# W_out's feature tiles half as seven block products, wider early weight fetches, buffers cleared by VectorE

## The chip, the cores and the metric

The kernel runs on one core of a Trainium2 chip. The core has a TensorE (matrix products, PE in the rows), a VectorE (DVE), a ScalarE (ACT), a GpSimd (POOL) and a SyncE (SP) that issues the DMA transfers. What is measured is the device time of one execution in microseconds (us); the kernel before takes 538.59 us in the median of three runs.

## The reference

Three parts follow each other: causal attention, a gated feed-forward layer with a root-mean-square norm ahead of it, and a bilinear layer.

```python
# q, k, v: (2, 12, 448, 64); x: (896, 768) after attention
scores = scale * np.matmul(q, k.transpose(0, 1, 3, 2))     # causal mask, then softmax
attn_out = np.matmul(attn, v)
...
rms = np.sqrt(np.mean(x * x, axis=-1, keepdims=True) + 1e-06)
xn = x / rms * rms_g
g = xn @ w_gate                                            # 768 -> 1536
val = xn @ w_val                                           # 768 -> 1536
x = g * (1.0 / (1.0 + np.exp(-g))) * val @ w_out           # 1536 -> 768
...
a = x @ w1                                                 # 768 -> 1024
b = x @ w2
h = a * b @ w3                                             # 1024 -> 1024
out = h @ w_out                                            # 1024 -> 768
```

## The kernel before

Everything is held with features on the 128 partitions and the 448 tokens of one batch row along the free axis. A float32 operand is split into a 16-bit high part and a 16-bit low part, and a product is three matmuls: high by high, high by low, low by high. So every product of a 128 by 128 weight tile with 448 tokens is three matmuls of 448 columns.

The weights come as 64-bit words. `fetch` issues the DMA on SyncE, unpacks the word with three passes (L462 on VectorE, L465 on ScalarE or L467 on VectorE, L469 on VectorE), and `halve` makes the high part (L445 on ScalarE or L446 on VectorE) and the low part (L449 on VectorE). `load_w` is both.

The last two weights are independent of the tokens and are multiplied first: `w_prime` computes W' = w3 times the last w_out, in matmuls of 384 columns, while the attention runs. It fetches w_out in pieces 384 columns wide and w3 in pieces 512 wide.

Most later products use a seven-product scheme for two-by-two blocks (Strassen-Winograd): the two batch rows of tokens are one block axis, two halves of the output or input features the other. `unit` prepares a weight's seven block combinations (two fetches of 768, four sums by VectorE, the halves), `mix` the seven combinations of the activations (`part` makes the two halves of one), and `wino` runs the seven products through PSUM banks, with three copies between banks by ScalarE (`fork`, L859) and two sums by VectorE (`join`, L864). The gate stage has 12 such groups (one for each feature tile f of 1536), the w1/w2 stage 8, the last stage 3.

W_out, between gate and w1/w2, is not done in this way: for each of the six output tiles d and each batch row, 12 feature tiles times three matmuls go into one bank, 432 matmuls of 448 columns in all, and its weight comes in 12 fetches of 768 columns.

```python
        for b in range(B):
            pr = T2 + (q + b / 2) * step
            ps, kp = mm_b.next()
            terms = []
            for f in range(NF):
```

The order of all instructions is decided before they are issued. `Plan.add` notes each piece of work with its engine, an estimated duration, what it reads and writes and a priority; `Plan.schedule` places the pieces on a timeline, and `Plan.order` issues them in the order of that timeline. The priorities are sums of the constants at the top (TP, WP0, WPS, GVS, OS, AS, FS and the table PO). Where that timeline leaves TensorE idle by more than 0.3 us in its first 50 us, pairs of matmuls with no use are put in, called fillers here (L435, 252 columns each). Each engine runs its own list in order and waits for the others by semaphores.

At the start VectorE clears `zero` (which the fillers read), and GpSimd clears and fills the masks (`masks`) and then the identity, the pads of `vh`, `pB` and `tB` (`pads`).

Of the kernel before, what the change touches and what calls it, by code (L numbers as in the profile page):

```python
# [18 lines left out]
P = 128  # L19
# [21 lines left out]
TP = 28.2101  # L41
WP0 = -128.5418
WPS = 43.0076
GVS = -29.6299
OS = -20.1067
AS = 4.781
FS = -7.5297
PO = dict(dq=-213.4192, dv=276.1722, vh=102.5046, vl=144.5046, sc=-0.1481, s3=-108.5638, hA=-122.7468,
    hl=86.4469, hB=-304.4551, pv=217.9082, sq=148.6883, nm=50.454, wm=-18.9366, ww=44.0488, wx=446.4336,
    g=314.9881, a=147.5041, o=-146.2756, f=300.9707, gm=162.7087, e=-116.3983, ae=122.9146, y=214.6087,  # L50
    t1=120.1752, mx=-49.7567, fk=-118.0695, pm=373.8229, dw=68.9952)
# [9 lines left out]
ARENA = 177152  # L61
# [177 lines left out]
LAT = {"pe": 0.25, "sp": 2.6, "dve": 0.12, "act": 0.12, "pool": 0.12}  # L239
# [32 lines left out]
def dma_us(b):  # L272
    return b / 335.0e3 + 0.1
# [3 lines left out]
def fused_kernel(ctx: ExitStack, tc, qk, v, g, wgv, wo, wab, w3t, wout, out):  # L277
# [61 lines left out]
    early = Ring("att", "se", 6, [P, 512, 2], I32), Ring("att", "ce", 6, [P, 512], I32)  # L339
# [37 lines left out]
    ew_r = Ring("late", "ew", 5, [P, S], F32)  # L377
    kp_r = Ring("late", "kp", 6, [P, S], F32)
    un = []
    for r in range(3):  # L380
        if r == 2:
# [3 lines left out]
          for f in range(NF) for b in range(B) for j in range(2)}  # L385
    wo_r = Ring("late", "wo", 3, [P, 2, DF], F16, [(j, c) for j in range(2) for c in range(2)])
# [12 lines left out]

    def abset(s, i, j):  # L400
        return ab[s, i, j], ("ab", s, i, j)

    def masks():
        nc.gpsimd.memset(mask, 0.0)
# [4 lines left out]
        nc.gpsimd.memset(mask3, 0.0)  # L409
# [6 lines left out]

    def pads():
        nc.gpsimd.memset(mhalf, -0.5)
        nc.gpsimd.memset(ident, 0.0)
# [4 lines left out]
        for t in vh_r.tiles:  # L424
            nc.gpsimd.memset(t[:, :, D:D + 1], 1.0)
        for i in range(2):
            nc.gpsimd.memset(pB_r.tiles[i][:, S:], 0.0)
            nc.gpsimd.memset(tB_r.tiles[i][:, :, :, 128:192], 0.0)

    add("pool", 2.5, masks, w=["mask"], prio=-10)  # L430
    add("pool", 1.6, pads, w=["mhalf", "ident"] + [(n, i) for n in ("vh", "pB", "tB") for i in range(2)], prio=1)

# [8 lines left out]
    add("dve", 0.54, lambda: nc.vector.memset(zero, 0.0), w=["zero"], prio=-10)  # L441
# [9 lines left out]

    def fetch(src, n, prio, rings=(st_r, cv_r)):
# [3 lines left out]
        (st, ks), (cv, kc) = (r.next() for r in rings)  # L456
# [4 lines left out]
            out=st, in_=src.bitcast(I32).rearrange("p (n t) -> p n t", t=2)), w=[ks], prio=prio + PO["dw"])  # L461
# [29 lines left out]
    def third(it, c, prio):  # L491
        cs = slice(c * 512, c * 512 + 512)
        load_w(w3[it][:, 0, cs], w3[it][:, 1, cs].bitcast(BF16), w3t[it][:, cs], 512, prio,
               [("w3", it, j, c) for j in range(2)], early)

    def w_prime():
        for nh in range(2):
            sl = slice(nh * 384, nh * 384 + 384)
            p0 = WP0 + nh * (6 + NI * WPS)
            for kt in range(NI):  # L500
                load_w(wo2[0][:, kt], wo2[1][:, kt], wout[kt][:, sl], 384, p0 + kt + PO["ww"], [("wb", 0, kt), ("wb", 1, kt)], early)
                if nh == 0 and kt % 4 == 3:
                    third(0, kt // 4, p0 + kt + 0.5 + PO["ww"])
            for it in range(NI):
                pr = p0 + 6 + it * WPS
                if nh == 0 and it:
                    for c in range(2):
                        third(it, c, pr + PO["wx"])
# [284 lines left out]
    def flat(t):  # L793
        return t.rearrange("p a c -> p (a c)")
# [222 lines left out]
```

## Time and profile before

| what | us |
|---|---|
| median of 3 runs | 538.59 (538.3 to 539.44) |
| the profiled execution | 538.64 |
| its span, first to last instruction | 536.9 |
| TensorE busy | 527.0 |
| VectorE busy | 458.9 |
| ScalarE busy | 402.7 |
| GpSimd busy | 6.8 |

The span is 1.7 us shorter than the profiled execution's own time; that remainder lies around it. Matmuls overlap, so TensorE's busy time says only that one was in flight; how fast they follow each other is read from the chain that ended last and from the count in a window. The mean duration of an instruction on VectorE or ScalarE includes up to 0.1 us in which the next has already begun.

### The profile page before, as it was taken

How to read it: one execution, taken by the hardware profiler on the slowest of the kernel's cores; microseconds unless marked ns; L12 is line 12 of the kernel's file. 1: busy time of each engine (PE TensorE's matmuls, PEld its weight loads, DVE VectorE, ACT ScalarE, POOL GpSimd, SP SyncE). 2: the span in 40 equal slices, each digit the busy share in tenths (PEclk: the TensorE clock that was granted, in tenths of full speed). 3: DMA queues.
4: the chain of work that ended last, by engine and by line, in shares of the span. 5: the costliest groups of instructions: out<-in, count | busy, mean ns of one | idle time of the engine just before them, and what ended most of it. 6: DMA issues, size and time to landing. Idle time of an engine off the chain costs nothing.

```text
span 536.9 us, 9199 instructions
## 1 busy us (share of the span) xinstructions
PE 527.0 (98%) x3514; PEld 293.0 (55%) x3514; DVE 458.9 (85%) x919; ACT 402.7 (75%) x629; POOL 6.8 (1%) x20
## 2 busy tenths in 40 slices
PE   9899999999998999999999999999999999999997
PEld 6566556666765455455555555555555555555553
DVE  6999999999989999999999963439999999999520
ACT  6999999999886887967779854547886878564431
POOL 3000000000000000000000000000000000000000
PEclk9999999999999999999999999999999999999999
DMA  8888669999931253334533671003532231000111
GB/s 311 278 314 284 184 209 200 252 194 204 170 118 60 80 199 133 118 118 142 208 119 132 242 276 59 1 1 119 177 118 93 84 118 59 2 0 18 51 70 68
DMA packets 46811, 74.90 MB, mean 140 GB/s; under 512 B 31408, under 2 KB 32944, under 8 KB 46768
## 3 DMA queue, kind: packets, MB, share of 16 engines
q1 hardware_dynamic: 46768, 74.33, 45.2%
q8 instruction: 27, 0.44, 0.3%
q14 instruction: 16, 0.13, 0.1%
HBM read 64.23 MB, written 2.75 MB: 125 GB/s over the span
## 4 chain that ended last, share of the span: by engine, by line
PE 79%; DVE 11%; ACT 6%; DMA 2%; issue 1%; ACTq 0%
PE bank L486 78%; DVE arena L449 4%; ACT arena L465 2%; DVE arena L469 2%; DVE arena L483 1%; PE bank L600 1%; DMA arena<-in_wgv 1%; ACT arena L445 1%; DVE arena L705 1%; DVE arena L462 1%; ACT arena L564 1%; DVE arena L864 1%; DMA arena<-in_wout 1%; ACT arena L736 1%; DVE arena L883 0%
## 5 line engine op out<-in xcount | busy, mean ns | idle before, releaser
L486 PE MATMUL bank<-arena 128*128 128x448 f16 (+7 forms) x2976 | 443.3, 315 | 3.2 <-DVE arena L560 0.7
L486 PEld LDWEIGHTS <-arena 128*128 128x128 bf16 (+1 forms) x3052 | 248.9, 98 | 217.6 <-issue 18.1
L449 DVE TENSOR_TENSOR arena<-arena 128x448 bf16<-128x448 f32 (+5 forms) x210 | 167.5, 811 | 18.8 <-ACT arena L445 17.5
L445 ACT ACTIVATE arena<-arena 128x448 f16<-128x448 f32 (+5 forms) x207 | 146.7, 726 | 40.0 <-PE bank L486 15.0
L465 ACT ACTIVATE arena<-arena 128x768 uint16<-128x768 uint16 (+2 forms) x76 | 122.9, 1632 | 21.6 <-DVE arena L462 17.8
L469 DVE SCALAR_TENSOR_TENSOR arena<-arena 128x768 int32<-128x768 int32 (+2 forms) x84 | 69.0, 825 | 10.4 <-ACT arena L465 9.5
L486 PE MATMUL bank<-xs,arena 128*128 128x448 f16 x364 | 75.1, 352 | 1.7 <-DVE arena L705 1.0
L483 DVE TENSOR_TENSOR arena<-arena 128x384 f32<-128x384 f32 (+1 forms) x131 | 72.8, 574 | 3.8 <-ACT arena L920 3.7
L859 ACT ACTIVATE bank<-bank 128x448 f32<-128x448 f32 x69 | 38.1, 555 | 22.5 <-PE bank L486 14.7
L864 DVE TENSOR_TENSOR arena<-bank,arena 128x448 f32<-128x448 f32 x46 | 28.4, 619 | 23.6 <-ACT bank L859 16.1
L462 DVE TENSOR_SCALAR arena<-arena 128x768 int32<-128x768 int32 (+2 forms) x84 | 41.4, 499 | 6.6 <-DMA arena<-in_wout 3.3
L564 ACT ACTIVATE arena<-arena 128x256 f32<-128x256 f32 (+3 forms) x84 | 41.5, 519 | 1.7 <-DVE arena L560 1.4
L837 ACT ACTIVATE arena<-bank 128x448 f32<-128x448 f32 x49 | 26.0, 541 | 22.2 <-PE bank L486 17.4
L560 DVE CUSTOM_DVE_ANT_0 arena<-bank,arena 128x384 f32<-128x384 f32 (+3 forms) x84 | 36.1, 444 | 2.5 <-PE bank L486 1.4
L486 PEld LDWEIGHTS bank<-arena 64*128 64x128 f32 (+2 forms) x288 | 26.4, 178 | 14.9 <-issue 4.2
L435 PE MATMUL bank<-arena 128*128 128x252 f16 x94 | 14.0, 308 | 1.1 <-DVE arena L441 1.1
L605 DVE TENSOR_TENSOR arena<-bank,arena 128x512 bf16<-128x512 f32 x20 | 13.3, 681 | 0.0
L920 ACT ACTIVATE arena<-bank 128x448 f32<-128x448 f32 x12 | 6.8, 562 | 8.4 <-PE bank L486 8.0
L883 DVE TENSOR_TENSOR arena<-bank,arena 128x448 f32<-128x448 f32 x20 | 12.3, 617 | 0.7 <-PE bank L486 0.6
L600 PE MATMUL bank<-arena 128*128 128x128 f32 x80 | 12.2, 279 | 0.3 <-ACT arena L564 0.3
L435 PEld LDWEIGHTS <-arena 128*128 128x128 f16 x94 | 10.0, 111 | 4.4 <-DVE arena L441 1.1
L603 ACT ACTIVATE arena<-bank 128x512 f16<-128x512 f32 x20 | 11.8, 602 | 0.3 <-PE bank L600 0.3
(46 smaller groups left out, 148.8 us busy)
## 6 DMA issues: line engine op xcount, KB each, us to landing
arena<-in_wgv SPq DMA_DIRECT2D x24, 768.0 KB, 4.5
arena<-in_wab SPq DMA_DIRECT2D x16, 768.0 KB, 4.4
arena<-in_wo SPq DMA_DIRECT2D x12, 768.0 KB, 4.9
arena<-in_w3t SPq DMA_DIRECT2D x16, 512.0 KB, 6.0
arena<-in_wout SPq DMA_DIRECT2D x16, 384.0 KB, 4.2
arena<-in_qk SPq DMA_DIRECT2D x12, 448.0 KB, 4.2
arena<-in_v SPq DMA_DIRECT2D x12, 256.0 KB, 3.5
out_t<-arena SPq DMA_DIRECT2D x12, 224.0 KB, 1.9
```

Source lines behind the costliest of these rows:

```text
L445: add("act", act_us(n), lambda: nc.scalar.activation(hi, src, AF.Copy), r=r, w=w, prio=prio, alt=(("dve", dve2_us(n), lambda: nc.vector.te ...
L449: add("dve", dve_us(n), lambda: nc.vector.tensor_tensor(lo, src, hi, op=ALU.subtract), r=r, w=w, prio=prio, port=True)
L462: add("dve", dve2_us(n), lambda: nc.vector.tensor_scalar(cv, hi, 3, 0x3FFFFFFF, op0=ALU.logical_shift_left, op1=ALU.bitwise_and), r=[ks], ...
L465: add("act", ACT_TOP * n - 0.08, lambda: nc.scalar.activation(b[:, :, 2], b[:, :, 1], AF.Copy, scale=1.0 / 8192, bias=-8191.0 / 16384), w= ...
L469: add("dve", dve_us(n), lambda: nc.vector.scalar_tensor_tensor(cv, hi, -0x3FFFFFF9, cv, op0=ALU.bitwise_and, op1=ALU.bitwise_or), r=[ks], ...
L483: add("dve", dve_us(n), lambda: nc.vector.tensor_tensor(out, a, b, op=op), port=True, **kw)
L486: nc.tensor.matmul(*a, **k)
L560: add("dve", dve_us(w), lambda: nc.vector.tensor_tensor_reduce(out=sc[:, :w], in0=ss[:, :w], in1=m, scale=-CSC, scalar=3.0e38, op0=ALU.add ...
L564: add("act", act_us(w) + 0.1, lambda: nc.scalar.activation(dst, sc[:, :w], AF.Exp, bias=mx[:, c:c + 1], scale=-1.0), r=[ksc, kmx + (c,)], ...
L837: add("act", actp_us(S), lambda: nc.scalar.activation(dst, ps[:, :S], func), r=[kp, *r], w=[kd], prio=p)
L859: add("act", actp_us(S), lambda: nc.scalar.activation(dst[0][:, :S], src[0][:, :S], AF.Copy), r=[src[1]], w=[dst[1]], prio=p + PO["fk"])
L864: add("dve", dve_us(S), lambda: nc.vector.tensor_tensor(d, ps[:, :S], m3, op=ALU.add), r=[kp, k3], w=[kd], prio=p)
```

## The change

Four edits are made together. (1) Six of W_out's 12 feature tiles, in three pairs (`KA`, `KB`), go as `wino` groups: three groups q, each with seven products of three tiles; the other six tiles (`KP`) are added straight into the same banks (`rest`, `more`). The activations of the paired tiles get their seven combinations by `mix` in the gate stage, and W_out's weight is fetched as three `unit`s and six pieces of 768. (2) `w_prime` fetches w_out as two 384-column tiles in one (768 wide) and w3 1024 wide. (3) What GpSimd cleared is cleared by VectorE, GpSimd keeps the selects; ScalarE runs a two-column Exp at the start; the first q and k transfer is split in two. (4) All priorities and some estimated durations of the planner have new numbers, and several rings of buffers have other sizes. TensorE's list has 27 matmuls of 448 columns fewer (1948 to 1921) and 16 fillers more (94 to 110).

```diff
-TP = 28.2101
-WP0 = -128.5418
+TP = 47.6981
+WP0 = -167.2566
...
+KA, KB = (0, 2, 4), (1, 3, 5)
+KP = tuple(f for f in range(NF) if f not in KA + KB)
...
-    early = Ring("att", "se", 6, [P, 512, 2], I32), Ring("att", "ce", 6, [P, 512], I32)
+    early = Ring("att", "se", 3, [P, DF2, 2], I32), Ring("att", "ce", 3, [P, DF2], I32)
...
-    ew_r = Ring("late", "ew", 5, [P, S], F32)
-    kp_r = Ring("late", "kp", 6, [P, S], F32)
+    ew_r = Ring("late", "ew", 4, [P, S], F32)
+    kp_r = Ring("late", "kp", 5, [P, S], F32)
...
-    wo_r = Ring("late", "wo", 3, [P, 2, DF], F16, [(j, c) for j in range(2) for c in range(2)])
+    wo_r = Ring("late", "wo", 2, [P, 2, len(KP) * P], F16, [(j,) for j in range(2)])
...
+    def clear():
+        nc.vector.memset(mask, 0.0)
+        nc.vector.memset(mask3, 0.0)
+        nc.vector.memset(ident, 0.0)
...
+    add("act", 1.5, lambda: nc.scalar.activation(junk[:, 0, :2], zero[:, :2], AF.Exp), r=["zero"], w=["junk"], prio=-10)
...
+    def last(kt, sl, prio):
+
+        (st, ks), (cv, kc) = (r.next() for r in early)
+        w = fetch(wout[kt:kt + 2, :, sl], 768, prio, ((st, ks), (cv, kc)))[0]
+        halve(768, flat(wo2[0][:, kt:kt + 2]), flat(wo2[1][:, kt:kt + 2]), w, kc,
+              [[("wb", j, k) for k in (kt, kt + 1)] for j in range(2)], prio)
...
-    def wino(w, x, n, pr):
+    def wino(w, x, n, pr, rest=None):
...
+        def more(dst, m, b):
+            if rest:
+                mm_group(*dst, rest(m, b), 3, pr, False)
+
         prod(1, 1, B, False, pr)
+        more(B, 0, 0)
...
+            part(e, ke, hwset, int(f in KB), i, pr)
+            if f in KB:
+                mix(hwset, i, *row, (e, ke), (g1, kg1), pr + PO["hm"])
...
+    for q in range(3):
+        pr = T2 + 2 * q * step
+        unit(wo[q], q, pr + PO["ou"])
...
+        (y0_, k0), (y2_, k2), c12, c22 = wino(uw(q), hwset, len(KA), pr, rest)
```

ScalarE's list, at its very start, of before (L465 unpacks a weight, L445 makes a high part, L564 is a softmax exponential, L603 copies transposed weights of the attention out of PSUM):

```order
L1013 UNCONDITIONAL_BRANCH
L465 ACT_TABLE_LOAD
L465 ACTIVATE arena<-arena 128x384
L445 ACTIVATE arena<-arena 128x384
L564 ACTIVATE arena<-arena 128x128 x2
L465 ACTIVATE arena<-arena 128x384
L564 ACTIVATE arena<-arena 128x256
```

And of after (L444 is the small Exp, L482, L457 and L592 answer to L465, L445 and L564):

```order
L1056 UNCONDITIONAL_BRANCH
L444 ACT_TABLE_LOAD
L444 ACTIVATE arena<-arena 128x2
L482 ACTIVATE arena<-arena 128x768
L592 ACTIVATE arena<-arena 128x128 x2
L457 ACTIVATE arena<-arena 128x768
L592 ACTIVATE arena<-arena 128x256 x2
```

The table load stands ahead of the small Exp and no longer ahead of the first weight, and the first two weight passes are twice as wide.

GpSimd's list at the start, of before:

```order
L404 MEMSET arena 128x512
L405 ISA
L405 AFFINE_SELECT arena<-arena 128x512
L409 MEMSET arena 128x448
L412 AFFINE_SELECT arena<-arena 64x448 x2
L418 MEMSET mhalf 128x4
L419 MEMSET arena 128x128
L420 AFFINE_SELECT arena<-arena 128x128
L425 MEMSET arena 128x8 x2
L427 MEMSET arena 128x64
L428 MEMSET arena 128x8x64
```

And of after:

```order
L423 ISA
L423 AFFINE_SELECT arena<-arena 128x512
L429 AFFINE_SELECT arena<-arena 64x448 x2
L433 AFFINE_SELECT arena<-arena 128x128
L437 MEMSET mhalf 128x4
```

All of its clears but that of `mhalf` have gone to the head of VectorE's list, ahead of VectorE's first weight pass.

VectorE's list while TensorE is in W_out, of before (L462 and L469 unpack, L449 is a low part, L483 a sum of `mix`):

```order
L469 SCALAR_TENSOR_TENSOR arena<-arena 128x768
L462 TENSOR_SCALAR arena<-arena 128x768
L469 SCALAR_TENSOR_TENSOR arena<-arena 128x768
L449 TENSOR_TENSOR arena<-arena 128x768
L483 TENSOR_TENSOR arena<-arena 128x448
L469 SCALAR_TENSOR_TENSOR arena<-arena 128x768
L449 TENSOR_TENSOR arena<-arena 128x448
```

And of after (L889 is a `join`, L500 a sum, L461 a low part, L479 and L486 unpack):

```order
L461 TENSOR_TENSOR arena<-arena 128x768
L889 TENSOR_TENSOR arena<-bank_62,arena 128x448
L461 TENSOR_TENSOR arena<-arena 128x448
L889 TENSOR_TENSOR arena<-bank_67,arena 128x448
L500 TENSOR_TENSOR arena<-arena 128x448
L479 TENSOR_SCALAR arena<-arena 128x768
L500 TENSOR_TENSOR arena<-arena 128x448
L461 TENSOR_TENSOR arena<-arena 128x448
```

The joins are new there: before, VectorE read no PSUM bank in this stage.

## Rows read from the trace of the kernel before

**Rows 1.** Page, part 1: busy time, share of the span, instructions.

```profile
PE 527.0 (98%) x3514; PEld 293.0 (55%) x3514; DVE 458.9 (85%) x919; ACT 402.7 (75%) x629; POOL 6.8 (1%) x20
```

**Rows 2.** Chain that ended last: start, duration, what.

```profile
223.36 310.03 PE bank L486 x1638
533.41 0.54 ACT arena L837
```

**Rows 3.** Groups by form: the matmul of 448 columns; busy, mean ns.

```profile
L486 PE MATMUL bank<-arena 128*128 128x448 f16 x1056 | 291.9, 352 | 0.6 <-ACT bank L859 0.4
```

**Rows 4.** Windows: length, busy of PE, PEld, DVE, ACT, POOL, clock, DMA share, GB/s.

```profile
150.00:500.00 350.00, 347.07 (x1869) 182.37 (x1865) 310.60 (x501) 250.77 (x349) 1.01 (x1) 1.00 0.31 105
150.00:225.00 75.00, 72.07 (x415) 40.17 (x411) 71.60 (x121) 60.49 (x91) 1.01 (x1) 1.00 0.35 119
225.00:300.00 75.00, 75.00 (x399) 38.77 (x397) 73.29 (x111) 58.62 (x83) 0.00 (x0) 1.00 0.43 151
300.00:375.00 75.00, 75.00 (x398) 38.80 (x397) 45.28 (x68) 41.65 (x46) 0.00 (x0) 1.00 0.29 103
```

**Rows 5.** VectorE's waits from 300 to 400 us: waited for, total, times, longest.

```profile
DVE arena L449 <- ACT arena L445: 14.8, 8, 3.6
```

**Rows 6.** Groups by form on VectorE in the later stages.

```profile
L483 DVE TENSOR_TENSOR arena<-arena 128x448 f32<-128x448 f32 x51 | 31.2, 616 | 3.8 <-ACT arena L920 3.7
L483 DVE TENSOR_TENSOR arena<-arena 128x384 f32<-128x384 f32 x80 | 43.4, 548 | 0.0
L449 DVE TENSOR_TENSOR arena<-arena 128x768 bf16<-128x768 f32 x46 | 43.8, 953 | 14.1 <-ACT arena L445 13.4
L449 DVE TENSOR_TENSOR arena<-arena 128x1536 bf16<-128x1536 f32 x20 | 35.1, 1753 | 1.2 <-ACT arena L445 1.1
L469 DVE SCALAR_TENSOR_TENSOR arena<-arena 128x768 int32<-128x768 int32 x52 | 49.3, 954 | 8.7 <-ACT arena L465 8.2
L462 DVE TENSOR_SCALAR arena<-arena 128x768 int32<-128x768 int32 x52 | 28.4, 552 | 3.2 <-DMA arena<-in_wab 2.2 <-DMA arena<-in_wgv 0.6
L864 DVE TENSOR_TENSOR arena<-bank,arena 128x448 f32<-128x448 f32 x46 | 28.4, 619 | 23.6 <-ACT bank L859 16.1 <-PE bank L486 6.4 <-ACT arena L837 0.9
```

**Rows 7.** Groups by form on VectorE for the early weights.

```profile
L462 DVE TENSOR_SCALAR arena<-arena 128x384 int32<-128x384 int32 x16 | 6.5, 410 | 3.4 <-DMA arena<-in_wout 3.3
L469 DVE SCALAR_TENSOR_TENSOR arena<-arena 128x384 int32<-128x384 int32 x16 | 8.8, 550 | 1.7 <-ACT arena L465 1.4
L449 DVE TENSOR_TENSOR arena<-arena 128x384 bf16<-128x384 f32 x36 | 19.5, 549 | 0.1
L449 DVE TENSOR_TENSOR arena<-arena 128x512 bf16<-128x512 f32 x23 | 15.6, 683 | 0.1
L449 DVE TENSOR_TENSOR arena<-arena 128x1024 bf16<-128x1024 f32 x6 | 7.3, 1219 | 1.2 <-ACT arena L445 1.2
```

**Rows 8.** Timeline of the first 8 us: start, duration, instruction, idle before.

```profile
0.84 0.22 DVE L441 MEMSET arena<- 128x190 uint32 x1 [0.84 <-PEq L1005]
4.37 1.27 DVE L462 TENSOR_SCALAR arena<-arena 128x384 int32<-128x384 int32 x1 [3.31 <-DMA arena<-in_wout]
4.42 1.28 ACT L465 ACT_TABLE_LOAD   x1 [4.42 <-DMA arena<-in_wout]
4.90 0.52 POOL L428 MEMSET arena<- 128x512 f16 x1
5.71 1.06 ACT L465 ACTIVATE arena<-arena 128x384 uint16<-128x384 uint16 x1
```

**Rows 9.** Timeline of TensorE: the last long row of fillers.

```profile
21.91 2.31 PE L435 MATMUL bank<-arena 128*128 128x252 f16 x20
```

**Rows 10.** Page, part 6: two DMA issues, KB each, median us to landing.

```profile
arena<-in_wgv SPq DMA_DIRECT2D x24, 768.0 KB, 4.5
arena<-in_wout SPq DMA_DIRECT2D x16, 384.0 KB, 4.2
```

More of the change, by code (lines that the diff above doesn't have):

```diff
@@ L398, in hset, with hwset @@
         return hb[b, f, j], ("h", b, f, j)
+    def hwset(s, i, j):
+        return hw[s, i, j], ("hw", s, i, j)
     def abset(s, i, j):
         return ab[s, i, j], ("ab", s, i, j)
+    def clear():
+        nc.vector.memset(mask, 0.0)
+        nc.vector.memset(mask3, 0.0)
+        nc.vector.memset(ident, 0.0)
+        for t in vh_r.tiles:
+            nc.vector.memset(t[:, :, D:D + 1], 1.0)
+        for i in range(2):
+            nc.vector.memset(pB_r.tiles[i][:, S:], 0.0)
+            nc.vector.memset(tB_r.tiles[i][:, :, :, 128:192], 0.0)
     def masks():
-        nc.gpsimd.memset(mask, 0.0)
         nc.gpsimd.affine_select(
@@ L423, in pads @@
         )
[L424 to L431, printed above, removed]
+        nc.gpsimd.memset(mhalf, -0.5)
+    cleared = [(n, i) for n in ("vh", "pB", "tB") for i in range(2)]
+    add("dve", 0.24, lambda: nc.vector.memset(zero, 0.0), w=["zero"], prio=-10)
+    add("dve", 1.7, clear, r=["zero"], w=["mask", "ident", *cleared], prio=-9)
+    add("pool", 2.3, masks, w=["mask", "ident", "mhalf"], prio=-10)
+    add("act", 1.5, lambda: nc.scalar.activation(junk[:, 0, :2], zero[:, :2], AF.Exp), r=["zero"], w=["junk"], prio=-10)
     def filler():
@@ L450, in lo_part, with flat @@
             port=True)
+    def flat(t):
+        return t.rearrange("p a c -> p (a c)")
     def fetch(src, n, prio, rings=(st_r, cv_r)):
-        (st, ks), (cv, kc) = (r.next() for r in rings)
+        (st, ks), (cv, kc) = ((r if isinstance(r, tuple) else r.next()) for r in rings)
         st, cv = st[:, :n], cv[:, :n]
@@ L499, in w_prime @@
             p0 = WP0 + nh * (6 + NI * WPS)
[L500 to L503, printed above, removed]
+            for kt in range(0, NI, 2):
+                last(kt, sl, p0 + kt + PO["ww"])
+                if nh == 0 and kt == 2:
+                    third(0, p0 + kt + 0.5 + PO["ww"])
             for it in range(NI):
@@ L506, in w_prime @@
                 if nh == 0 and it:
-                    for c in range(2):
-                        third(it, c, pr + PO["wx"])
+                    third(it, pr + PO["wx"])
                 ps, kp = g_b.next()
@@ new lines, in fused_kernel, with rest @@
+    for q in range(3):
+        pr = T2 + 2 * q * step
+        unit(wo[q], q, pr + PO["ou"])
+        wp = []
+        for m in range(2):
+            wt, kw = wo_r.next()
+            load_w(wt[:, 0], wt[:, 1].bitcast(BF16), wo[q, 2 + m], len(KP) * P, pr + m * step + PO["o"],
+                   [kw + (j,) for j in range(2)])
+            wp.append((wt, kw))
+        def rest(m, b, wp=wp):
+            (wt, kw), terms = wp[m], []
+            for n, f in enumerate(KP):
+                cs = slice(n * P, n * P + P)
+                (h0, kh0), (h1, kh1) = hset(b, f, 0), hset(b, f, 1)
+                terms.append((((wt[:, 0, cs], wt[:, 1, cs].bitcast(BF16)), (h0, h1)), [kw + (0,), kw + (1,), kh0, kh1]))
+            return terms
+        (y0_, k0), (y2_, k2), c12, c22 = wino(uw(q), hwset, len(KA), pr, rest)
+        pr += PO["y"]
+        c11, c21 = kp_r.next(), kp_r.next()
+        copy_out(*c11, y0_, k0, pr)
+        part(*c11, xs, 0, q, pr)
+        copy_out(*c21, y2_, k2, pr)
+        part(*c21, xs, 1, q, pr)
+        mix(xs, q, c11, c12, c21, c22, pr)
```

104 lines of the change are left out of this document (45 added, 59 removed).

## The prediction

> **What bounds the kernel now.** I read the page's busy shares first, then the chain that ended last, then windows, then the timeline of the start. The shares put TensorE at 98% and VectorE at 85% [rows 1], but TensorE's share only says that some matmul was in flight. The chain tells more: from 223.36 us on it is one piece, 310.03 us of matmuls, 1638 of them [rows 2], so 310.03 / 1638 = 0.1893 us each. At the full TensorE clock of 2.4 GHz, which the windows show as granted throughout (1.00 in the clock column [rows 4]), 448 columns are 448 / 2400 = 0.1867 us. The matmuls therefore follow each other with nearly nothing between them, while each lasts 0.352 us by its own row [rows 3] because two overlap. For 310 of 537 us no other engine holds TensorE up. After its last matmul there is one copy of 0.54 us at 533.41 [rows 2] and the transfer out, neither of which the change touches. Everything in the change is therefore to be asked two things: does it take matmuls off TensorE's list, and does the other engines' work still arrive in time.
>
> For the second, the windows show who is near. From 225 to 300 us VectorE is busy 73.29 of 75 us, so it keeps TensorE fed with 1.7 us to spare; from 300 to 375 us it is busy only 45.28 us [rows 4]. In that later stretch it waits, among others 14.8 us in 8 waits for ScalarE's high parts [rows 5], and TensorE runs on: this is W_out, where there is much matmul work and little else. ScalarE has room in all of these windows.
>
> **Part 1: W_out by block products.** Three of the six pairs of feature tiles go from eight block products to seven. Before: 6 output tiles x 2 batch rows x 6 feature tiles x 3 matmuls = 216 for the tiles concerned. After: 3 groups x 7 products x 3 tiles x 3 matmuls = 189. That is 27 matmuls less, the count that the two lists show too, at 0.1893 us [rows 2]: 27 x 0.1893 = **5.1 us off TensorE**, all of it inside the unbroken chain, so it comes off the end unless something else becomes late.
>
> What it adds on VectorE, by rows 6:
> - Activations: for each of the three pairs four sums and three more low parts of 448, 7 x 0.616 = 4.31 us; three pairs 12.9 us.
> - Weights: a `unit` is two first passes of 768 (0.552), two second passes (0.954), low parts of 768 (0.953), 384 (0.549, [rows 7]) and 1536 (1.753), and four sums of 384 (0.548): 1.10 + 1.91 + 0.95 + 0.55 + 1.75 + 2.19 = 8.46 us. Three are 25.4 us. Six fetches of 768 go: 6 x (0.552 + 0.954 + 0.953) = 14.8 us. Net 10.6 us.
> - Joins: 6 x 0.619 = 3.7 us.
>
> Together 27.2 us, all of it between about 150 and 500 us. There VectorE was busy 310.60 of 350 us [rows 4], so it had 39.4 us free. After the change it has 310.6 + 27.2 = 337.8 us of work against 350 - 5.1 = 344.9 us of TensorE: 7.1 us free, 2.1%. In the stretch where it was already the nearest engine, 225 to 300 us, it stood idle 1.71 of 75 us, 2.3%, without holding TensorE up [rows 4]. At that share it needs 337.8 / 0.977 = 345.7 us, which is 0.8 us more than TensorE. At the share of 150 to 225 us, where it idled 3.40 of 75 us (4.5%) and TensorE was not quite full either (72.07 of 75), it would need 337.8 / 0.955 = 353.7 us, 8.8 us more. The other end is 0: VectorE works ahead where it can, and part 2 gives it back some time before 150 us. I take **+0.8 us**, since most of the stretch looks like 225 to 300 us and not like the change from norm to gate; 0 and +8.8 are the ends. A gain from this added work is excluded, because nothing on TensorE waits less for it. On ScalarE three copies between banks and some high parts come to each group; its 250.77 of 350 us [rows 4] hide them.
>
> **Part 2: wider early fetches.** Two passes of 384 become one of 768, and that saves the fixed part: on VectorE 2 x (0.410 + 0.550 + 0.549) = 3.02 us become 0.552 + 0.954 + 0.953 = 2.46 us [rows 6, 7], 0.56 us less in each of 8. Two low parts of 512 at 0.683 become one of 1024 at 1.219 [rows 7], 0.15 us less; the second pass of the fetch is alike and the first saves more, as it does at 768, so about 0.45 us less in each of 8. VectorE has some 8 us less to do before 150 us. Nothing there is on the unbroken chain, so I count it as cover for part 1 and not as a gain. In return the first piece is later: a fetch of 768 KB lands 4.5 us after its issue where one of 384 KB took 4.2 [rows 10], and its ScalarE pass lasts twice as long as the 1.06 us of now [rows 8].
>
> **Part 3: the start.** At present the first weight arrives at 4.4 us and two things then happen at once. VectorE's first pass takes 1.27 us [rows 8] instead of the 0.410 that is its mean [rows 7]; GpSimd is clearing a buffer at that time (0.52 us from 4.90). ScalarE loads its function table for 1.28 us, and the weight's second pass starts at 5.71 [rows 8]. After the change both are out of the way: ScalarE loads the table while the first transfer is on its way, and the clears have gone to VectorE. These are some ten instructions; the one clear that the trace shows on VectorE took 0.22 us for 190 columns [rows 8], so at most about 2 us, in the 3.31 us in which VectorE waits for the first landing. GpSimd's selects now wait for these clears and no longer stand in GpSimd's own queue behind them; the first softmax pass comes only after 7 us. So up to 1.28 us may come off the start.
> The Trainium skill (ScalarE: Activation LUTs, What ACT_TABLE_LOAD costs) gives 2.66 us for such a load, drain included; the trace shows 1.28 us and then 0.01 us to the next ScalarE instruction, so at this place I go by the row. By the page this end would be 2.66 us.
>
> Against it stands what the new order does. TensorE's list has 16 fillers more, all in the first 50 us. The last long row of fillers took 2.31 us for 20 [rows 9], 0.116 each; 16 of them are 1.9 us. They mark where the planner saw TensorE with nothing to do: W' begins behind two pairs of heads now, not behind one. The ends are -1.3 and +1.9 us; I take **+0.8 us**, nearer to the fillers, because the wider first passes take back much of what the table load gives.
>
> **Part 4: numbers and rings.** The new priorities cost nothing by themselves. Fewer buffers (e.g. two for W_out's pieces in place of three, five in place of six for results) make VectorE's work ahead shorter; that lies in the +8.8 end of part 1. Splitting the first q and k transfer lets the first scores start on 128 columns and adds one issue on a queue that then waits for buffers anyway: nothing.
>
> **The sum.** 538.64 (the profiled execution, practically the median of 538.59) - 5.1 + 0.8 + 0.8 = **535.1 us**.
>
> **The rivals.**
> - *VectorE becomes the bound* from gate to w1/w2. For it: 2.1% of free time is less than it ever shows in a full window. Against: from 300 to 375 us its waits were those of an engine with nothing due. At 4.5% idle it costs 8.8 us: 538.64 - 5.1 + 0.8 + 8.8 = 543.1, slower. It decides the sign from the point where the idle share passes 3.6%: then 337.8 / 0.964 = 350.4 us is 5.5 us more than TensorE's 344.9 and eats the gain.
> - *The start is worse than its fillers say*: W' waits for four wide w_out pieces and a wide w3 piece in ScalarE's queue, and TensorE loses the time of one W' column group more, 24 matmuls of 384 columns, estimated from 0.1893 at 448 as 24 x 0.162 = 3.9 us, in place of 0.8. That gives 538.2, about the same.
> - *The relief before 150 us counts*: VectorE arrives at the gate stage early, nothing of part 1 is late, and the table load comes off in full: 538.64 - 5.1 - 1.3 = 532.2.
> - *TensorE is not the limit*, so that 27 matmuls less bring nothing and only the two charges stay: 540.2. The weight loads are busy only 38.77 of 75 us in a full window [rows 4]. The pace of 0.1893 us against 0.1867 [rows 2] speaks clearly against it. The Trainium skill (Perfetto Trace Analysis, Identifying the Most-Contended Engine) would judge TensorE's headroom by that share of weight loads, which is 52% here; the trace's pace does not agree that there is room.
>
> **How the numbers follow.** My forecast has 0.60, the early arrival 0.14, VectorE as the bound 0.12, the worse start 0.12, TensorE not the limit 0.02. The range reaches from the early-arrival case, less 0.4 for the scatter of runs, 531.8, to 539.6: it holds the forecast, the early arrival, the worse start and the milder part of the VectorE case. A measurement can tell about 0.2% from no change, which is 1.1 us, so faster means under 537.5 and slower over 539.7. Faster: 0.60 less 0.02 for its own upper end, 0.14, and a quarter of the worse start, 0.75 in all. Same: the rest of the worse start and the gentle part of the VectorE case, 0.14. Slower: 0.11.
>
> **What would show it.** Part 1: the last stretch again one chain of matmuls at 0.189 us, 27 fewer in all. The VectorE case: gaps on TensorE that `join`, `mix` or low parts end, between 200 and 450 us, with VectorE at 96% or more and TensorE's matmul count in a 75 us window under 398. Part 3: the first weight pass on ScalarE right behind VectorE's first pass, which is back at its row's length; and the last filler not later than TensorE's useful work pays for. It is wrong if TensorE's unbroken chain begins much later than 223 us.

## The result, and the profile after

The changed kernel takes **533.66 us** (median of 4 executions, 532.32 to 534.58), the kernel before beside it 538.68 us (538.3 to 539.44). The ratio is 0.9905, with a 95% interval of 0.989 to 0.9919: 5.0 us faster. The profiled execution is the one of 534.58 us, the longest of the four, with a span of 532.8 us; it is 4.1 us shorter than the profiled execution of before.

The page of after, part 1, as [rows 1]:

```profile
PE 523.7 (98%) x3503; PEld 292.1 (55%) x3503; DVE 478.5 (90%) x923; ACT 410.3 (77%) x615; POOL 4.8 (1%) x11
```

TensorE's share is unchanged, VectorE's rose from 85% to 90%. The chain that ended last, from 163.94 us on (start, duration, what), as [rows 2]:

```profile
163.94 0.04 ACTq L738
163.98 0.05 issue
164.03 0.63 ACT arena L738
164.66 0.47 ACT arena L457
165.13 0.53 ACT arena L764
165.66 0.03 issue
165.69 1.29 DVE arena L733 x2
166.97 0.02 issue
167.00 0.63 ACT arena L738
167.63 0.44 ACT bank L884
168.08 0.04 issue
168.12 361.27 PE bank L503 x1900
529.39 0.02 issue
529.41 0.54 ACT arena L862
```

Before, the unbroken piece of matmuls began at 223.36 us; now it begins at 168.12. Between the norm and the end nothing holds TensorE up in this execution. The windows, as [rows 4] (length, busy of PE, PEld, DVE, ACT, POOL, clock, DMA share, GB/s):

```profile
150.00:500.00 350.00, 347.93 (x1859) 183.13 (x1858) 332.49 (x536) 263.93 (x371) 1.25 (x1) 1.00 0.31 105
150.00:225.00 75.00, 72.93 (x405) 40.86 (x404) 70.64 (x115) 60.51 (x92) 1.25 (x1) 0.98 0.31 105
225.00:300.00 75.00, 75.00 (x399) 38.80 (x397) 73.42 (x117) 64.26 (x88) 0.00 (x0) 1.00 0.37 127
300.00:375.00 75.00, 75.00 (x398) 38.79 (x397) 70.56 (x109) 53.19 (x69) 0.00 (x0) 1.00 0.46 158
```

TensorE starts 399 and 398 matmuls in the two full windows, as before. VectorE has filled the stretch from 300 to 375 us: 70.56 us where it had 45.28. Its joins are new (groups by form, 150 to 500 us; out<-in, count | busy, mean ns | idle before):

```profile
L889 DVE TENSOR_TENSOR arena<-bank,arena 128x448 f32<-128x448 f32 x48 | 29.7, 622 | 5.4 <-PE bank L503 3.2 <-ACT bank L884 1.9 <-ACT arena L862 0.3
```

**Where the 5 us lie.** The first matmul that reads `xs` (the gate's product) starts at 156.37 us before and at 156.50 after. From it to the last matmul it takes 376.65 us before (to 533.02) and 372.52 after (to 529.02). So in this pair start and attention gave +0.1 us and the later stages -4.1 us. The latter holds -5.1 for 27 matmuls and +1.7 for a fall of the clock that follows here; the remaining -0.7 is a difference that was not measured. Of it 0.3 us are waits: after the gate's first product TensorE stands 2.36 us before and 2.07 after.

Traces of the changed kernel's order without that fall settle the later stages better. In `late_table`, `low_cleared` and `busy_norm` (below) the clock stays at 1.00 and the same distance is 371.6 us each time, 5.1 us less than before, although in the first two TensorE's waits are 0.3 us longer than before's; with the fall it is 372.5 to 372.7 (after, `clears_pool`, `low_twice`). The distance ahead of the gate is less certain than +0.1 suggests: in five other traces, which up to there have after's order or differ from it in the start alone (`sums3`, `sums7`, `busy_norm`, `clears_pool`, `late_table`), the gate's first product starts between 154.67 and 155.83 us.

The fall of the clock, in three windows of after (columns as above):

```profile
164.00:168.00 4.00, 2.05 (x17) 1.67 (x16) 2.54 (x5) 3.09 (x7) 0.00 (x0) 1.00 0.01 3
168.90:172.30 3.40, 3.40 (x11) 1.36 (x10) 2.71 (x6) 1.55 (x5) 0.00 (x0) 0.50 0.02 5
172.00:176.00 4.00, 4.00 (x22) 2.00 (x20) 3.62 (x6) 4.00 (x4) 0.00 (x0) 0.96 0.01 2
```

TensorE's timeline in front of the fall (start, duration, instruction, idle before):

```profile
163.75 1.95 PE L503 MATMUL bank<-arena 128*128 128x128 f32 x16
166.43 0.35 PE L503 MATMUL bank<-xs,arena 128*128 128x448 f16 x1 [0.73 <-DVE arena L733]
168.12 3.18 PE L503 MATMUL bank<-xs,arena 128*128 128x448 f16 x10 [1.34 <-ACT bank L884]
```

Between 165.7 and 168.1 us TensorE had one matmul, while it waited for the norm's chain above. From 168.9 to 172.3 us the granted clock is 0.50 (1.2 GHz), and TensorE starts 11 matmuls in 3.40 us where 18 go at 0.189: 3.4 us at half speed cost 1.7 in this place. In the profiled execution of before TensorE was hardly busier there (2.26 us between 164 and 168, in place of 2.05), yet the clock stayed at 1.00. `late_table` has the same two waits, of 0.73 and 1.34 us, and no fall either; there TensorE waits once more, for a copy between banks:

```profile
167.06 2.05 PE L503 MATMUL bank<-xs,arena 128*128 128x448 f16 x10 [1.34 <-ACT bank L884]
168.00:172.00 4.00, 4.00 (x23) 2.08 (x22) 4.00 (x8) 2.81 (x4) 0.00 (x0) 1.00 0.02 4
178.21 1.86 PE L503 MATMUL bank<-arena 128*128 128x448 f16 x9 [0.59 <-ACT bank L884]
```

With the fall TensorE comes later and that wait of 0.59 us is gone. So at the end the fall costs 372.5 - 371.6 = 0.9 us and not 1.7.

### The profile page after: what moved, and what is told of

Read it like the earlier page. It is cut to its first block, busy times and chain, and to the rows that moved or that the text cites. A ratio compares the mean times of both kernels' runs of the same rounds, so it can differ in the third digit from the quotient of the medians.

```text
span 532.8 us, 9142 instructions
## 1 busy us (share of the span) xinstructions
PE 523.7 (98%) x3503; PEld 292.1 (55%) x3503; DVE 478.5 (90%) x923; ACT 410.3 (77%) x615; POOL 4.8 (1%) x11
## 4 chain that ended last, share of the span: by engine, by line
PE 84%; ACT 6%; DMA 4%; DVE 4%; issue 1%; ACTq 0%; DVEq 0%; SPq 0%
PE bank L503 83%; DMA arena<-arena 4%; ACT arena L482 2%; ACT arena L592 1%; PE bank L628 1%; ACT arena L457 1%; DVE arena L461 1%; DMA arena<-in_wout 1%; DVE arena L588 1%; DVE arena L486 1%; PE bank L448 0%; DVE arena L633 0%; DVE arena L479 0%; ACT arena L631 0%; DVE arena L733 0%
## 5 line engine op out<-in xcount | busy, mean ns | idle before, releaser
L503 PE MATMUL bank<-arena 128*128 128x448 f16 (+10 forms) x2949 | 437.3, 315 | 2.4 <-ACT wpr L542 0.9
L461 DVE TENSOR_TENSOR arena<-arena 128x448 bf16<-128x448 f32 (+5 forms) x206 | 174.2, 865 | 5.5 <-ACT arena L457 5.2
L457 ACT ACTIVATE arena<-arena 128x448 f16<-128x448 f32 (+5 forms) x203 | 151.6, 773 | 31.4 <-DVE arena L500 13.1
L482 ACT ACTIVATE arena<-arena 128x768 uint16<-128x768 uint16 (+1 forms) x60 | 119.2, 1995 | 15.3 <-DVE arena L479 14.3
L500 DVE TENSOR_TENSOR arena<-arena 128x384 f32<-128x384 f32 (+1 forms) x155 | 87.5, 581 | 0.2
L503 PE MATMUL bank<-xs,arena 128*128 128x448 f16 (+1 forms) x364 | 75.4, 356 | 2.1 <-ACT bank L884 1.3
L486 DVE SCALAR_TENSOR_TENSOR arena<-arena 128x768 int32<-128x768 int32 (+1 forms) x68 | 67.0, 987 | 5.0 <-ACT arena L482 4.4
L889 DVE TENSOR_TENSOR arena<-bank,arena 128x448 f32<-128x448 f32 x52 | 32.2, 622 | 23.4 <-ACT bank L884 17.6
L592 ACT ACTIVATE arena<-arena 128x256 f32<-128x256 f32 (+3 forms) x84 | 41.5, 519 | 0.2 <-DVE arena L588 0.2
L479 DVE TENSOR_SCALAR arena<-arena 128x768 int32<-128x768 int32 (+1 forms) x68 | 38.7, 571 | 3.4 <-DMA arena<-in_wout 3.1
L588 DVE CUSTOM_DVE_ANT_0 arena<-bank,arena 128x128 f32<-128x128 f32 (+3 forms) x84 | 36.6, 449 | 2.7 <-PE bank L503 2.2
L701 ACT ACTIVATE arena<-arena 128x128 bf16<-128x128 f32 (+2 forms) x20 | 9.1, 453 | 2.3 <-DVE arena L693 2.2
```

The costliest lines, as they stand in the source:

```text
L457: add("act", act_us(n), lambda: nc.scalar.activation(hi, src, AF.Copy), r=r, w=w, prio=prio, alt=(("dve", dve2_us(n), lambda: nc.vector.te ...
L461: add("dve", dve_us(n), lambda: nc.vector.tensor_tensor(lo, src, hi, op=ALU.subtract), r=r, w=w, prio=prio, port=True)
L479: add("dve", dve2_us(n), lambda: nc.vector.tensor_scalar(cv, hi, 3, 0x3FFFFFFF, op0=ALU.logical_shift_left, op1=ALU.bitwise_and), r=[ks], ...
L482: add("act", ACT_TOP * n - 0.08, lambda: nc.scalar.activation(b[:, :, 2], b[:, :, 1], AF.Copy, scale=1.0 / 8192, bias=-8191.0 / 16384), w= ...
L486: add("dve", dve_us(n), lambda: nc.vector.scalar_tensor_tensor(cv, hi, -0x3FFFFFF9, cv, op0=ALU.bitwise_and, op1=ALU.bitwise_or), r=[ks], ...
L500: add("dve", dve_us(n), lambda: nc.vector.tensor_tensor(out, a, b, op=op), port=True, **kw)
```

## The experiments

Each ran beside the kernel before; ratios are to it, and "after" is the changed kernel, at 0.9905.

**1. W_out's product undone: `no_blocks`, `no_blocks_fit`, `no_blocks_old`.** All three keep the wide fetches and the new start, and compute W_out directly as before. The diff against after, shortened:

```diff
-    wo_r = Ring("late", "wo", 2, [P, 2, len(KP) * P], F16, [(j,) for j in range(2)])
+    wo_r = Ring("late", "wo", 3, [P, 2, DF], F16, [(j, c) for j in range(2) for c in range(2)])
...
-        (y0_, k0), (y2_, k2), c12, c22 = wino(uw(q), hwset, len(KA), pr, rest)
...
+            mm_group(ps, kp, terms, 6, pr)
```

They differ in the numbers that set the order: those of after in the first, numbers fitted anew to this list of work in the second, those of the kernel before in the third.

> The changed kernel with W_out as in the kernel before (432 matmuls, twelve fetches of 768); the wide fetches, the start and the new numbers stay. If the 27 matmuls are the gain (27 x 0.1893 = 5.1 us), it takes about 538.8 us, 1.000 of the kernel before, and the matmuls follow each other as closely as before. Rival, that the new numbers and the start brought the gain and the added VectorE work eats what the matmuls save: 533 to 535 us, 0.990 to 0.993, with VectorE about 20 us less busy.

Measured: 541.84 us, ratio 1.0054 [1.0039, 1.0069], 3 us above what the 27 matmuls explain.

> The kernel before with the wide fetches and the new start, its own W_out (no block products) and its own numbers. If the gain of the change is the 27 matmuls, this takes the time of the kernel before, 538 to 539 us. If the start and the fetches are worth what the run with the old start suggests, it is faster than the kernel before, 533 to 536 us. If numbers have to be fitted anew for every change of the lists, it is slower, 540 to 543 us, as the run without blocks at the new numbers was (541.84), with the loss between 0 and 200 us.

Measured: 542.39 us, ratio 1.0062 [1.0041, 1.0082], slower than the kernel before, although this kernel has the same products and priorities, with the wide fetches and the new start. It also has the rings and the planner's estimated durations of after.

> The changed kernel with W_out's product done directly again, as in no_blocks, but with priorities fitted to this list of work. It separates the 27 matmuls from the order. Theory 1 (the gain is the 27 matmuls less): 27 x 0.189 = 5.1 us more than after, so about 538.8 us, level with the kernel before, and TensorE from 150 to 200 us busy about 47 to 48 of 50 us as in after, where no_blocks had 46.09. Rival (wide fetches, the new start and the new fit make the gain): 533 to 536 us. If it stays at 541 to 542 us, the 3 us that no_blocks lost beyond the matmuls are not a matter of the fit.

Measured: 537.39 us (10 executions), ratio 0.9986 [0.9976, 0.9997]. Only this one has an order fitted to its own work, as after has; how near either fit is to the best one isn't known. By the ratios W_out by block products is worth (0.9986 - 0.9905) x 538.5 = 4.4 us, with intervals that hold 5.1; all the rest of the change together is worth 0.8 us. None of the ten executions has a mean clock under 0.999 and three of after's four have 0.997, so the 4.4 us hold a fall of 0.9 us: without it some 5.3 us, an estimate. In its trace the gate's first product and the last matmul are 376.4 us apart, as before (376.65), against 371.6 with block products and no fall.

The other two lost 4 to 5 us more. `no_blocks` ends in one chain of 349.19 us for 1845 matmuls from 187.67 us on, `no_blocks_fit` in one of 351.02 us for 1854 from 181.00, the same pace, so that the loss of `no_blocks` against it lies ahead of these chains. A part is seen in the window from 150 to 200 us, the first line of `no_blocks_old`, the second of `no_blocks`, the third of `no_blocks_fit`:

```profile
150.00:200.00 50.00, 45.61 (x290) 26.82 (x288) 46.76 (x78) 37.88 (x62) 1.30 (x1) 1.00 0.29 96
```

```profile
150.00:200.00 50.00, 46.09 (x276) 26.81 (x273) 46.38 (x82) 39.23 (x62) 1.76 (x1) 1.00 0.32 109
```

```profile
150.00:200.00 50.00, 47.19 (x270) 26.88 (x269) 47.42 (x79) 39.81 (x63) 1.37 (x1) 1.00 0.32 111
```

TensorE stands 4.4, 3.9 and 2.8 us in the norm (after: 47.93 busy, 2.1 us). Another part is in the first 100 us, where TensorE is busy 93.8 us in `no_blocks_old`, 96.4 in `no_blocks` and 97.8 in `no_blocks_fit`, fillers included; the rest was not followed.

**2. The numbers alone: `old_numbers`, `old_start`.** The first is after with the priorities of the kernel before:

```diff
-TP = 47.6981
-WP0 = -167.2566
+TP = 28.2101
+WP0 = -128.5418
...
```

> The changed kernel with the priorities of the kernel before (the two new ones kept): block products, wide fetches, new start. Matmuls alone: 538.6 - 5.1 = 533.5 us if the new numbers bring nothing. If the fit is a part of the gain, 536 to 542 us, with TensorE's waits in the first 200 us, above all at the norm.

Measured: 540.0 us, ratio 1.0024 [1.0011, 1.0038]. All of the change is in it but the fitted priorities, and it is slower than before: the order is worth 6.3 us to this kernel, falls of the clock included (nine of its ten executions have a mean clock of 0.992 to 0.997). The second puts GpSimd's clears back and takes the small Exp out, with after's numbers; the planner then gives another order throughout:

```diff
-        nc.vector.memset(mask, 0.0)
-        nc.vector.memset(mask3, 0.0)
...
+        nc.gpsimd.memset(mask, 0.0)
...
+        nc.gpsimd.memset(mask3, 0.0)
...
-    add("act", 1.5, lambda: nc.scalar.activation(junk[:, 0, :2], zero[:, :2], AF.Exp), r=["zero"], w=["junk"], prio=-10)
```

> The changed kernel with the clears on GpSimd again and without the small Exp, so that the table load stands ahead of the first weight pass. If the start is on the path with its table load (1.28 us) and the slow first VectorE pass (1.27 in place of 0.57), 1.3 to 2 us more: about 535 to 536 us. Rival, that later fillers and waits absorb it: 533.5 to 534.2 us, with the first W' groups ending at most 0.5 us later.

Measured: 542.25 us, ratio 1.0059 [1.0042, 1.0077]: a miss for both sides. It doesn't measure the start, as the norm shows (150 to 200 us, then 172 to 180):

```profile
150.00:200.00 50.00, 43.98 (x294) 25.93 (x292) 46.90 (x77) 41.16 (x68) 1.25 (x1) 0.93 0.33 107
172.00:180.00 8.00, 6.20 (x20) 2.41 (x20) 7.97 (x13) 6.17 (x12) 0.00 (x0) 0.58 0.08 31
```

TensorE stands 6 us there, and the clock falls for longer. Nor is the start the old one: a softmax exponential now stands first on ScalarE, so the table load is early again, and VectorE's first weight pass comes at 8.49 us, behind GpSimd's last clear, at its fast length:

```profile
0.73 1.28 ACT L589 ACT_TABLE_LOAD   x1 [0.73 <-PEq L1045]
4.92 0.53 POOL L437 MEMSET arena<- 128x512 f16 x1
8.49 0.56 DVE L476 TENSOR_SCALAR arena<-arena 128x768 int32<-128x768 int32 x1 [1.62 <-DMA arena<-in_wout]
```

The start had to be tried with the order held still.

**3. The start with the order held: `clears_pool`, `late_table`.** Only the engine of the clears, and only the early Exp, are put back; TensorE's list stays row for row that of after.

```diff
-            nc.vector.memset(t[:, :, D:D + 1], 1.0)
+            nc.gpsimd.memset(t[:, :, D:D + 1], 1.0)
...
```

```diff
-    add("act", 1.5, lambda: nc.scalar.activation(junk[:, 0, :2], zero[:, :2], AF.Exp), r=["zero"], w=["junk"], prio=-10)
+    add("act", 1.5, lambda: None, r=["zero"], w=["junk"], prio=-10)
```

> The changed kernel with the clears on GpSimd in place of VectorE and nothing else: TensorE's, ScalarE's and SyncE's lists are word for word those of the changed kernel. If the start is on the path with GpSimd's clears, which are under way when VectorE's first weight pass runs, that pass takes about 1.3 us again in place of 0.57 and the first weight is 0.7 us later: 534.2 to 534.6 us. Rival, that the 8.6 us of the run with the old start came from its new order alone: 533.4 to 533.9 us. A third reading, that the clears delay everything behind them: over 536 us.

Measured: 533.77 us, 0.9907 [0.9886, 0.9929].

> The changed kernel without the small Exp, so that the function table is loaded ahead of the first weight pass of ScalarE; all other lists are those of the changed kernel. If the load is on the path, 1.28 us minus what waits anyway, at most 1.3 us: up to 535 us. Rival, that ScalarE catches up because it waits for VectorE's passes later: 533.4 to 533.9 us. In either case far under the 542.25 us of the run with the old start, if that came from its new order.

Measured: 533.67 us, 0.9898 [0.9879, 0.9916]. Neither can be told from after, and in neither trace is the gate's first product later than after's 156.50 us (155.60 and 155.44). In after's first 8 us the load is early and VectorE's first pass is fast (start, duration, instruction, idle before), as [rows 8]:

```profile
0.73 1.28 ACT L444 ACT_TABLE_LOAD   x1 [0.73 <-PEq L1048]
5.52 0.56 DVE L479 TENSOR_SCALAR arena<-arena 128x768 int32<-128x768 int32 x1 [3.06 <-DMA arena<-in_wout]
6.12 1.91 ACT L482 ACTIVATE arena<-arena 128x768 uint16<-128x768 uint16 x1 [3.89 <-DVE arena L479]
```

The first weight now lands 1.15 us later (VectorE begins at 5.52, not 4.37), and ScalarE's pass ends at 8.03 for 768 columns, where before it ended at 6.77 for 384.

`late_table` does put the load back behind the landing, and ScalarE's first pass starts 0.76 us later:

```profile
5.59 1.28 ACT L482 ACT_TABLE_LOAD   x1 [5.59 <-DMA arena<-in_wout]
6.88 1.91 ACT L482 ACTIVATE arena<-arena 128x768 uint16<-128x768 uint16 x1
```

`clears_pool` does not bring VectorE's slow pass back. GpSimd is through with its large clears at 2.98 us, and the pass takes 0.56 us as in after:

```profile
2.46 0.52 POOL L420 MEMSET arena<- 128x512 f16 x1
5.59 0.56 DVE L479 TENSOR_SCALAR arena<-arena 128x768 int32<-128x768 int32 x1 [4.53 <-DMA arena<-in_wout]
```

So its unchanged time says that the engine of the clears doesn't matter here, and nothing of what a slow first pass would cost.

**4. How near VectorE is to the bound: `sums7`, `sums3`.** Sums of weights are done twice, the second time writing the same values, with the order held: in the last four weights of the gate stage and W_out's three (28 passes of 0.548, 15.3 us), or in W_out's three alone (12 passes, 6.6 us).

```diff
-        unit(wgv[f], f % 3, pr + PO["g"])
+        unit(wgv[f], f % 3, pr + PO["g"], 2 if f > 7 else 1)
...
-        unit(wo[q], q, pr + PO["ou"])
+        unit(wo[q], q, pr + PO["ou"], 2)
```

> The changed kernel with each of the four sums of seven weights (the last four of the gate stage, the three of W_out) done twice in place, in the same order on every engine: 28 x 0.548 = 15.3 us more on VectorE between about 250 and 380 us. If VectorE is nearly the bound there, as the 2.1% of free time of the prediction say, TensorE waits for most of it: 541 to 548 us, with the chain passing through VectorE in that stretch. Rival, that its waits in that stretch are free time: under 1 us more, 533 to 535 us, and VectorE's idle time from 150 to 500 us falls by about 14 us from 17.5.

Measured: 546.34 us, 1.0141 [1.0123, 1.016]: 12.7 us more than after for 15.3 us of work.

> The changed kernel with every sum of W_out's three block-product weights done twice (the second writes the same values again): 12 more passes of about 0.548 us, 6.6 us on VectorE between 300 and 380 us, the order of everything else kept. That stretch has VectorE busy 70.56 of 75 us in after. Theory 1 (VectorE is within 2% of the bound there, as my prediction's second term had it, and sums7 lost 12.7 us of 15.3): 3 to 6.6 us slower than after, 536.7 to 540.3 us. Rival (there is room left for these weights, which are wanted last): under 1 us, 533.7 to 534.7 us.

Measured: 538.01 us, 0.9988 [0.9974, 1.0002]: 4.4 us more for 6.6. In both about 2.4 us were absorbed (15.3 - 12.7 = 2.6; 6.6 - 4.4 = 2.2). This is rough by about 1 us, since falls of the clock are in all these medians (0.997 or less in all four executions of `sums7` and in five of the ten of `sums3`). `sums7` from 275 to 350 us in windows of 25:

```profile
275.00:300.00 25.00, 22.35 (x116) 11.06 (x115) 24.35 (x41) 16.65 (x23) 0.00 (x0) 1.00 0.37 126
300.00:325.00 25.00, 21.76 (x112) 10.62 (x111) 24.53 (x39) 20.24 (x26) 0.00 (x0) 1.00 0.44 144
325.00:350.00 25.00, 22.88 (x113) 11.38 (x112) 22.02 (x35) 12.86 (x17) 0.00 (x0) 0.93 0.47 171
```

TensorE starts 112 to 116 matmuls where a full window has 134, VectorE is at 97% and 98% in the first two of them, and TensorE's waits there (225 to 400 us; waited for, total, times, longest) are for the copies between banks and for VectorE:

```profile
PE bank L503 <- ACT bank L884: 6.7, 6, 2.1
PE bank L503 <- DVE arena L461: 1.5, 4, 0.8
PE bank L503 <- DVE arena L889: 0.6, 1, 0.6
```

After has no wait of TensorE at all in that window. This is what the rival "VectorE becomes the bound" would have looked like; the changed kernel stays some 2 to 3 us short of it.

**5. VectorE ahead of the gate, more and less: `low_twice`, `low_cleared`.** In the first the low half of the eight early `w_out` pieces is computed twice; in the second those eight and the eight of `w3t` are set to zero and not computed. The order is held in both.

```diff
-              [[("wb", j, k) for k in (kt, kt + 1)] for j in range(2)], prio)
+              [[("wb", j, k) for k in (kt, kt + 1)] for j in range(2)], prio, 2)
```

```diff
-        add("dve", dve_us(n), lambda: nc.vector.tensor_tensor(lo, src, hi, op=ALU.subtract), r=r, w=w, prio=prio,
+        add("dve", dve_us(n), lambda: nc.vector.memset(lo.bitcast(I32), 0) if clear else nc.vector.tensor_tensor(lo, src, hi, op=ALU.subtract), r=r, w=w, prio=prio,
```

> The changed kernel with the low half of each of the eight early pieces of w_out done twice (the same values written again): 8 more passes of 0.953 us, 7.6 us on VectorE in the first 160 us, the order of everything else kept. Theory 1 (VectorE's work of the start lies beside the fetches and fillers, and only the stage from 150 us on is near the bound): under 1 us, 533.7 to 534.7 us. Rival (VectorE's work of the start is on the path to the attention weights' product): up to 7 us slower, 537 to 541 us, with the first gate matmul, at 156.50 us in after, later by as much.

Measured: 541.07 us, 1.0043 [1.0028, 1.0058]: 7.4 us more than after for 7.6 us of work. My theory fell; the first gate matmul comes 6.1 us later (162.59), and of the 6.3 us between the two profiled executions (540.84 and 534.58) that is nearly all.

> The changed kernel with the low halves of the early weights (eight w_out pieces of 768, eight w3t pieces of 1024) not computed but set to zero by VectorE, the order of all engines kept; that part of the computation is left out, so it is a time of less work. In the trace of after a clear of 256 words takes 0.272 us and one of 224 takes 0.245, which gives about 0.38 and 0.49 us for 384 and 512 in place of 0.953 and 1.226: 8 x 0.57 + 8 x 0.74 = 10.5 us less on VectorE before 156 us. Theory 1 (after low_twice: VectorE alone is the path up to the gate, in both directions): 8 to 10 us faster than after, 523.5 to 526 us. Rival (VectorE is only one of several engines that are full there, so that more work delays the end but less does not bring it nearer): 530 to 533 us, with new waits of TensorE on ScalarE's copies or on the transfers before 150 us. In between would mean that both hold in part.

Measured: 533.96 us, 0.9906 [0.9886, 0.9927]: nothing gained; the first gate matmul is at 156.70. The rival's mechanism is the nearer one, but its 530 to 533 us were missed, and the new waits of TensorE that it named did not come in sum: TensorE stands 3.5 us ahead of the gate in both kernels. The first 156.4 us of before, after, `low_twice` and `low_cleared`:

```profile
0.00:156.40 156.40, 152.35 (x1519) 97.06 (x1520) 145.51 (x425) 144.94 (x275) 6.84 (x20) 1.00 0.85 233
```

```profile
0.00:156.40 156.40, 152.84 (x1534) 98.22 (x1535) 145.09 (x391) 142.84 (x242) 4.80 (x11) 1.00 0.87 233
```

```profile
0.00:156.40 156.40, 148.90 (x1494) 95.08 (x1495) 146.82 (x388) 138.74 (x231) 3.54 (x10) 1.00 0.82 228
```

```profile
0.00:156.40 156.40, 152.93 (x1533) 98.48 (x1534) 136.70 (x391) 142.49 (x242) 4.80 (x11) 1.00 0.84 233
```

With 8.4 us less to do, VectorE only waits longer (for TensorE in the softmax passes, 7.2 us in 9 waits, where after has 2.2 in 5):

```profile
DVE arena L588 <- PE bank L503: 7.2, 9, 1.4
```

TensorE and ScalarE are as full as in after, and the DMA share is 0.84. So several engines are full there in a given order: a delay of VectorE was passed on nearly in full, and relief of it alone brought nothing. TensorE stands only 3.56 us there in after, and its held list keeps the 110 fillers, whether or not a weight comes sooner; whether an order fitted to the relief, with fewer of them, would gain was not tried.

**6. The clock: `busy_norm`.** After with matmuls put into TensorE's waits in the norm (4 and 7 of them, into a bank that is written anew later):

```diff
-            mm_group(*dst, terms, 3, p, fresh)
+            mm_group(*dst, terms, 3, p, fresh, (lambda: busy(7)) if dst is B else None)
```

> The changed kernel with 11 matmuls more (4 and 7, into a bank that is overwritten later) in the two waits of TensorE at the end of the norm, 165.7 to 168.1 us. If the fall of the granted clock to 0.5 from 168.9 to 172.3 us comes from those waits, the clock stays at 1.00 and the 1.7 us that half the clock costs in 3.4 us come back: about 532.0 us, 0.9875 of the kernel before. Rival, that the clock falls for another reason: it falls again, 533.7 to 534 us.

Measured: 532.42 us (532.19 to 534.18), 0.9887 [0.9867, 0.9906]. The window that held the near-idle stretch, and the next:

```profile
164.00:168.00 4.00, 3.98 (x24) 2.12 (x23) 2.74 (x5) 3.12 (x8) 0.00 (x0) 1.00 0.00 0
168.00:172.00 4.00, 4.00 (x23) 2.08 (x22) 4.00 (x8) 2.80 (x4) 0.00 (x0) 1.00 0.02 6
```

There is no fall, neither in the profiled execution nor by the mean clock in the other three. That the added matmuls prevent it is likely but not shown: `late_table` and `low_cleared` leave the waits empty and their traces have no fall either, and of the 16 executions of after, `clears_pool`, `late_table` and `low_cleared` eight have 0.997 and eight 1.0. This kernel has the lowest median of all that ran, 1.2 us under after; the two intervals overlap, and from the gate's first product to the last matmul its trace takes 371.6 us like those two, so that nothing but a fall avoided could be the gain.

## Why the prediction was right, point by point

- **27 matmuls at 0.1893 us: right.** The chain's pace is 361.27 us for 1900, the fall of the clock in it; without the fall's 1.7 us that is 0.1892 each. From the gate's first product to the last matmul, traces without a fall take 376.65 us before and 371.6 with the change, 5.1 us less. `no_blocks_fit` puts the product at 4.4 us with 5.1 inside the interval. The rival "TensorE is not the limit" is out.
- **VectorE's tie, +0.8: measured 0.** The added work was forecast at 27.2 us; between 150 and 500 us VectorE is busy 332.49 - 310.60 = 21.9 us more, and TensorE waits for nothing from 168 us on. The counts came out as forecast (joins 46 to 52, sums 51 to 63 and 80 to 92); why the busy time grew by less was not followed. From 225 to 300 us VectorE idles 1.58 of 75 us, 2.1%, so a share of idle time as small as the forecast's does hold. What was mis-sized is the reserve: 7.1 us was an average over 350 us, and the doubled sums found 2 to 3 us.
- **The start, +0.8: measured +0.1, and in five other traces a gate 0.5 to 1.7 us earlier than before's.** The two ends were taken from rows that show no cost or gain here: the table load's 1.28 us (`late_table`), and the 16 fillers (110 now, 94 before, and the same 156 us), which seem to fill time that TensorE had anyhow; no run took them out. The first landing was mis-sized too: by the medians of [rows 10] a wide piece was to land 0.3 us later, and VectorE began 1.15 us later. The Trainium skill (ScalarE: Activation LUTs, What ACT_TABLE_LOAD costs) would have had 2.66 us there. The rows again show 1.28 us with the next instruction right behind it, and `late_table` no loss in time that its scatter lets see.
- **Part 2 as cover and not as a gain: the value was right, the reason only half.** VectorE's busy time ahead of the gate is 145.1 us after 145.5, not 8 us less. The passes of the early weights did shrink, but VectorE took over clears from GpSimd (6.84 to 4.80 us) and passes from ScalarE (144.94 to 142.84 us). `low_cleared` shows that it didn't matter in this order: a relief of 8.4 us brings nothing. So the rival "the relief before 150 us counts" finds no support. That VectorE's work there is off the path, as "nothing there is on the unbroken chain" suggests, is wrong in the other direction, by `low_twice`. What the wide fetches are worth alone wasn't tried.
- **"The new priorities cost nothing by themselves": the weakest step, and luck.** They are worth 6.3 us to this kernel (`old_numbers`). The forecast came out because the numbers had been fitted to the new list, which it did not weigh; without that the same edits end slower than before, and none of the rivals priced that case.
- **Not forecast: the fall of the clock**, 1.7 us in its place and 0.9 at the end. That the forecast of 535.1 us lies only 1.4 us over the measured 533.66 is in part luck as well: it held two charges of 0.8 us that were not found, and lacked a fall that three of the four executions have.

## What to carry to other kernels

When an order is fitted to a list of work, undoing one edit without a new fit measures the fit: hold every engine's list still and change what one instruction does, or fit each variant, before an edit is credited. Count the work that comes off an unbroken chain at the chain's own pace, and test the engine beside it by doubling some of its passes, since its idle share averaged over a stage says little of its reserve. In a held order a stretch in which several engines are full can pass a delay of one of them on nearly in full and return no relief given to it alone, as the first 156 us did here.

## What was not expected of the hardware

After a stretch of about 2.4 us with a single matmul in it the granted clock fell to 0.50 for 3.4 us, while TensorE was busy throughout the fall; that cost 1.7 us in its place and 0.9 us at the end. It isn't in every execution: by the mean clock three of after's four have it (0.997) and the fourth doesn't (1.0, 532.32 us), and the profiled executions of `low_cleared` and `late_table`, with the same waits in the norm, keep 1.00. The kernel before is not free of it, by the same sign: of its 50 executions beside the experiments 16 have a mean clock of 0.996 or 0.997 and a median of 539.3 us, the other 34 one of 538.3. It explains a part of the scatter between executions only: `busy_norm` has one of 534.18 us at a mean clock of 1.0, which stays open. But for `low_twice`, traces of after's order begin the gate anywhere from 154.67 to 156.70 us, so a part of the scatter lies ahead of it.

VectorE's first pass took 1.27 us beside GpSimd's clear [rows 8] and 0.56 us for twice the columns without one. That the clear is the cause is not shown: no run brought the slow pass back, `old_start` and `clears_pool` included, so what it costs stays open too.
